# Global keys stored behind every third local key block of a windowed attention

## The chip, the core and the metric

The kernel runs on one core of one Trainium2 chip. The metric is the device time of one execution in microseconds (us), and less is better. The core has five engines with an instruction queue each: TensorE (PE, matrix products; its weight loads are listed apart as PEld), VectorE (DVE), ScalarE (ACT), GpSimd (POOL) and SyncE (SP). [...]

## The reference

Four batches of 8 heads have 512 local and 32 global tokens of width 64. A local query sees the 32 global keys and the local keys at most 32 places away; a global query sees everything. A dense squared-relu feed-forward layer and a layer of routed experts follow.

```python
k_all = np.concatenate([k_g, k_l], axis=2)
s_g = scale * np.matmul(q_g, k_all.transpose(0, 1, 3, 2))
out_g = np.matmul(sm(s_g), np.concatenate([v_g, v_l], axis=2))
s_ll = scale * np.matmul(q_l, k_l.transpose(0, 1, 3, 2))
mask = np.abs(pos[:, None] - pos[None, :]) <= 32
s_ll = np.where(mask, s_ll, -1000000000.0)
s_lg = scale * np.matmul(q_l, k_g.transpose(0, 1, 3, 2))
a_l = sm(np.concatenate([s_lg, s_ll], axis=-1))
out_l = np.matmul(a_l, np.concatenate([v_g, v_l], axis=2))
...
h = x @ w_in; r = np.maximum(h, 0.0); x2 = (r * r) @ w_out
# then: route each token of x2 to one of 8 experts, relu layer, gated sum
```

## The kernel before

**Stages.** The local queries are cut into 16 tiles t of 128 (tile t belongs to batch b = t // 4). `attention` (L392) makes one tile: scores, masked softmax, transposes, product with the values, transposition into the input of the feed-forward layer. `attention_global` (L478) makes the 32 global queries of a batch in two halves g of four heads. `ffn_block` runs the dense layer for two tiles at once (products h at L700 to L702, acc at L725 to L727; its first block works on plain, unsplit weights, L697 and L723). Then tokens are routed, and the expert layer fills the rest of the span.

**Order.** The order of the work is written out by hand in four strings of steps (`SEQ`, `EVEN`, `ODD`, `TAIL`); a letter stands for a step of a generator: `a` and `b` for attention tiles, `g` for global attention, `G` for the global keys, `0` to `3` for the key transposes of a head pair, `q` for queries, `E` and `F` for units of the dense layer, `V` for value loads, `W` for weight loads, `A` and `C` for conversions. Instructions of one engine run in the order in which the steps issue them.

**Keys.** `kT` of a batch holds the transposed keys of four head pairs, with the two heads of a pair in the two halves of 64 rows. `prep_k` (L326) makes four transposes for a head pair and one ACT copy (L331) of 128x512 elements into `kT`; `prep_globals` (L316) puts the 32 global keys behind the 512 local ones, in columns 512 to 543 (ACT copy, L320).

**Scores.** A tile is cut into four segments i of 32 queries. A segment sees a window of 96 local keys from `window(tt, i)` (L345) on, and the 32 global keys. So for a head pair p the loop at L404 makes, for both heads g, four products of 32 queries with 96 keys, and then four of 32 queries with 32 global keys: 64 products for a tile, all from L413. Each of the float32 products stands in the trace as two matmul records and two weight loads (128 records for a tile). The 4 segments write to the four quarters of 32 rows of the result, the 2 heads read the two halves of 64 rows.

**After the scores.** DVE adds one of three masks (L426; made by POOL at the start, L130 to L149, float32), takes the maximum, ACT makes the exponentials, PE transposes (L442), ACT or DVE copies, and PE multiplies with the value rows (`po`, L451). `load_v` (L353) fetches those rows: for each window one DMA for 96 local rows into rows 0 to 95 and one for the 32 global rows into rows 96 to 127. The first two tiles have places of their own (L369, L370), later windows rotate through six places `vr`, in which the global rows are loaded again only when the batch changes (L377, L380). All these DMAs are issued by SP.

**Global queries.** For each half, four products of 32 queries with 512 columns of `kT` (`gsa`) and four with 32 columns (`gsb`), L485.

Of the kernel before, what the change touches and what calls it, by code (L numbers as in the profile page):

```python
# [8 lines left out]
F32 = mybir.dt.float32  # L9
# [45 lines left out]
def attention_ffn_routed_experts(  # L55
# [73 lines left out]

    masks = {}  # L130
    for kind in range(3):
        m = const.tile([P, P], F32, name=f"mask{kind}")
        nc.gpsimd.memset(m, 0.0)
        for i in range(NQ):
            shift = 0
            if kind == 0 and i == 0:
                shift = SEG
            if kind == 2 and i == NQ - 1:
                shift = -SEG
            seg = m[SEG * i:SEG * (i + 1), 0:WIN]  # L140
            nc.gpsimd.affine_select(
                out=seg, in_=seg, compare_op=ALU.is_ge, fill=NEG,
                base=shift, pattern=[[1, WIN]], channel_multiplier=-1,
            )
            nc.gpsimd.affine_select(
                out=seg, in_=seg, compare_op=ALU.is_ge, fill=NEG,
                base=2 * SEG - shift, pattern=[[-1, WIN]], channel_multiplier=1,
            )
        masks[kind] = m  # L149
# [166 lines left out]
    def prep_globals(b):  # L316
        kT[b] = sb("kT", 1, [P, NPAIR, S], f"kT{b}")
        tr = pair(f"kgtr{b}")
        transposes(tr, kin[b, "g"][:, 0:DM], SG)
        nc.scalar.copy(kT[b][:, :, SL:S], tr[:, :, 0:SG])  # L320
        tr = pair(f"qgtr{b}")
        transposes(tr, kin[b, "g"][:, DM:2 * DM], SG)
        qgT[b] = sb("qgT", 1, [P, NPAIR, SG], f"qgT{b}")
        nc.scalar.copy(qgT[b], tr[:, :, 0:SG])

    def prep_k(b, p):  # L326
        tr = pair(f"ktr{b}_{p}")
        for j in range(TPB):
            two = kin[b, p // 2][:, j, 2 * (p % 2):2 * (p % 2) + 2, :]
            nc.tensor.transpose(tr[:, j, :], two.rearrange("p r d -> p (r d)"), ident)  # L330
        nc.scalar.copy(kT[b][:, p, 0:SL].rearrange("p (q j) -> p j q", j=TPB), tr)  # L331
# [13 lines left out]
    def window(tt, i):  # L345
        return min(max(tt * P + i * SEG - SEG, 0), SL - WIN)

    vin, vgl = {}, {}
    windows, opening, opening_places = [], [], []
    loaded = [0]  # L350
    globals_in = {}

    def load_v(t, part):  # L353
        if t >= NLT:
            return
        b, tt = divmod(t, TPB)
        for i in range(2 * part, 2 * part + 2):
            w0 = window(tt, i)
            if i and w0 == window(tt, i - 1):
                vin[t, i] = vin[t, i - 1]  # L360
                continue
            if t < 2:

                k, half = divmod(len(opening), 2)
                if half == 0:
                    opening_places.append(stage(f"v{k}"))
                w = opening_places[k][:, half * DM:(half + 1) * DM]
                opening.append(w)
                nc.sync.dma_start(heads(w[0:WIN]), v_l[b, :, w0:w0 + WIN, :].rearrange("h s d -> s h d"))  # L369
                nc.sync.dma_start(heads(w[WIN:P]), v_g[b].rearrange("h s d -> s h d"))  # L370
# [6 lines left out]
            nc.sync.dma_start(heads(windows[k][0:WIN]), v_l[b, :, w0:w0 + WIN, :].rearrange("h s d -> s h d"))  # L377
            if globals_in.get(k) != b:
                globals_in[k] = b
                nc.sync.dma_start(heads(windows[k][WIN:P]), v_g[b].rearrange("h s d -> s h d"))  # L380
            assert all(w is not windows[k] for w in vin.values())
            vin[t, i] = windows[k]
# [9 lines left out]
    def attention(t, S_TAG, O_TAG):  # L392
        b, tt = divmod(t, TPB)
        q = qT[t // 2][:, :, (t % 2) * P:(t % 2 + 1) * P]
        mask = masks[0 if tt == 0 else 2 if tt == TPB - 1 else 1]
# [10 lines left out]
        for p in range(NPAIR):  # L406
            for globals_ in (False, True):
                for i in range(NQ):
                    w0 = window(tt, i)
                    keys, cols = (slice(SL, S), slice(WIN, P)) if globals_ else (slice(w0, w0 + WIN), slice(0, WIN))  # L410
                    for g in range(2):
                        rows = slice(D * g, D * (g + 1))
                        nc.tensor.matmul(  # L413
                            scs[g][SEG * i:SEG * (i + 1), p, cols],
                            lhsT=q[rows, p, SEG * i:SEG * (i + 1)], rhs=kT[b][rows, p, keys],
                            start=True, stop=True,
                        )
# [4 lines left out]
        for g in range(2):  # L422
            if t != 1:
                sms[g] = sb("sm", 2, [P, S], f"sm{t}_{g}")[:, 0:4 * P]
# [53 lines left out]
    def attention_global(b, S_TAG, O_TAG):  # L478
        for g in range(2):
            sa = ps.tile([P, SL], F32, tag=S_TAG, bufs=BANKS[S_TAG], name=f"gsa{b}_{g}")  # L480
            sb_ = pair(f"gsb{b}_{g}")[:, 0, 0:SG]
            for o, c, n in ((sa, 0, SL), (sb_, SL, SG)):
                for hh in range(4):
                    p, r = divmod(4 * g + hh, 2)
                    nc.tensor.matmul(  # L485
                        o[SG * hh:SG * (hh + 1), :],
                        lhsT=qgT[b][D * r:D * (r + 1), p, :], rhs=kT[b][D * r:D * (r + 1), p, c:c + n],
                        start=True, stop=True,
                    )
# [5 lines left out]
            pg = sb("sm", 2, [P, S], f"pg{b}_{g}")  # L495
            rs = sb("osum", 2, [P, H], f"grs{b}_{g}")
            nc.scalar.activation(pg[:, 0:SL], sa, AF.Exp, bias=mx[:, 3:4], scale=SCALE, accum_out=rs[:, 0:1])
            nc.scalar.activation(pg[:, SL:S], sb_, AF.Exp, bias=mx[:, 3:4], scale=SCALE, accum_out=rs[:, 1:2])
# [5 lines left out]
            for c in range(TPB):  # L504
                nc.tensor.transpose(ptr[:, c, :], pg[:, 0:SL].rearrange("p (k j) -> p j k", j=TPB)[:, c], ident)
# [3 lines left out]
            nc.tensor.transpose(ptr[0:SG, 0, :], pg[:, SL:S], ident)  # L509
# [245 lines left out]
    def ffn_tile(t):  # L755
# [3 lines left out]
        place = sb("kT", 1, [P, NPAIR, S], f"g{t}").rearrange("p a s -> p (a s)")  # L759
# [181 lines left out]
    def wide_tile(e):  # L941
# [4 lines left out]
        def first(f):  # L946
# [8 lines left out]
            gl = sb("sm", 2, [P, S], f"ewgl_{e}_{f}")[:, 0:WIDE].bitcast(F32R)  # L955
# [23 lines left out]
        ys = sb("kT", 1, [P, NPAIR, S], f"ewys_{e}").rearrange("p a s -> p (a s)")[:, 0:KD * WIDE]  # L979
# [42 lines left out]
    def expert_tile(e, j, si):  # L1022
# [4 lines left out]
        hl = sb("kT", 1, [P, NPAIR, S], f"ehl_{name}").rearrange("p a s -> p (a s)")[:, 0:2 * KE * P].bitcast(F32R)  # L1027
# [8 lines left out]
        def first(fb, k0, k1):  # L1036
# [8 lines left out]
            if k1 == KD:  # L1045
                rs[fb] = sb("sm", 2, [P, S], f"er_{name}_{fb}")[:, 0:512]
                nc.scalar.activation(rs[fb], h, AF.Relu)
# [118 lines left out]
    def rest_tile(e, j, in_arm, o):  # L1166
# [13 lines left out]
        r = sb("sm", 2, [P, S], f"er_rest{e}")[:, 0:fw]  # L1180
# [31 lines left out]
    with tc.manual_schedule():  # L1212
# [48 lines left out]
        idle = sb("sm", 2, [P, S], "idle").bitcast(BF16)[:, 0:DM]  # L1261
# [50 lines left out]
        both = sb("kg", 1, [P, 2 * NSLOT], "slots", I32)  # L1312
# [96 lines left out]
        def more(e, j):  # L1409

            if j == UNROLL:
                with tc.For_i(UNROLL, (n_tok[e] + (P - 1)) // P, 1) as it:
                    gi = sb("gi", 2, [P, 1], f"gi{e}", I32)
# [190 lines left out]
```

## Time and profile before

| | us |
|---|---|
| median of 3 runs | 708.66 (707.76 to 709.51) |
| the profiled execution | 710.78 |
| its span in the trace | 709.1 |
| mean granted clock of TensorE | 0.98 |
| PE busy in the span | 683.5 (96%) |
| DVE / ACT / POOL busy | 396.2 / 365.5 / 163.7 |

The profiled execution is 2.1 us longer than the median, and 1.7 us of it lie outside the span. A row of the timeline is an engine's instructions of one form that run one after another: start, length, engine, line, tiles, shape and count; what stands in square brackets is the idle time before it and what ended that. The granted clock is a share: 1.00 is the higher of TensorE's two levels (2.4 GHz), 0.50 the lower (1.2 GHz).

### The profile page before, as it was taken

Reading aid. Unit: us, or ns where it says so; the run is one execution under the profiler, and the core shown is the slowest. Engines: PE = TensorE matmul, PEld = TensorE weight load, DVE = VectorE, ACT = ScalarE, POOL = GpSimd, SP = SyncE. Lnnn points to the kernel's source line nnn. Section 1 sums busy time; section 2 is a strip of 40 time slices with the busy share of each in tenths; the row PEclk is TensorE's granted clock in tenths of the full one; section 3 lists DMA queues with packets and bytes.
Section 4 is the critical chain, followed back from the end, with each engine's and each line's share of the span. In section 5 each row is a group of like instructions: output and inputs, shape, how many; then the busy total and the mean of one; then the engine's idle time right before and its main releaser. Section 6 shows DMA issues by size and latency. Waiting matters only on the chain. (4 is left out here: it accounts for less than half of the span.)

```text
span 709.1 us, 18592 instructions
## 1 busy us (share of the span) xinstructions
PE 683.5 (96%) x7621; PEld 574.3 (81%) x7621; DVE 396.2 (56%) x1073; ACT 365.5 (52%) x939; POOL 163.7 (23%) x205
## 2 busy tenths in 40 slices
PE   6789999999999999999999999999999999999996
PEld 4566668788888888988898888888887887898875
DVE  1879973873556166165516526544338733915984
ACT  5756557665535545453555545344434514515862
POOL 6000043354211121211221221122220432401311
PEclk8699999999999999999999999999999999999998
DMA  9999744056052501306350120410026588962920
GB/s 273 245 276 245 281 112 106 2 130 125 2 139 61 146 31 36 84 2 146 91 109 32 36 75 2 161 62 1 31 84 201 204 272 285 374 254 77 388 96 21
DMA packets 118758, 93.90 MB, mean 132 GB/s; under 512 B 84789, under 2 KB 91957, under 8 KB 118660
## 3 DMA queue, kind: packets, MB, share of 16 engines
q1 hardware_dynamic: 108352, 71.01, 35.9%
q10 hardware_dynamic: 8292, 15.48, 6.6%
q0 software_dynamic: 2016, 6.09, 2.5%
q8 instruction: 63, 1.03, 0.6%
q14 instruction: 35, 0.29, 0.1%
HBM read 80.31 MB, written 12.66 MB: 131 GB/s over the span
## 5 line engine op out<-in xcount | busy, mean ns | idle before, releaser
L184 POOL TENSOR_TENSOR gl<-g,gh 128x256 fp32r<-128x256 f32 x107 | 79.7, 745 | 302.8 <-ACT gh L183 142.3
L700 PE MATMUL h<-xh,w_in 128*128 128x256 f32 x464 | 134.9, 291 | 0.7 <-ACT xh L183 0.7
L701 PE MATMUL h<-xl,w_in 128*128 128x256 f32 x464 | 129.6, 279 | 0.3 <-DVE xl L184 0.3
L702 PE MATMUL h<-xh,w_in 128*128 128x256 f32 x464 | 129.7, 280 | 0.0
L725 PE MATMUL acc<-w_out,gh 128*128 128x512 f32 x232 | 97.5, 420 | 1.5 <-ACT gh L183 1.5
L727 PE MATMUL acc<-w_out,gl 128*128 128x512 f32 x232 | 91.9, 396 | 0.2
L726 PE MATMUL acc<-w_out,gh 128*128 128x512 f32 x232 | 91.6, 395 | 0.0
L700 PEld LDWEIGHTS h<-xh,w_in 128*128 128x128 f32 x464 | 87.1, 188 | 4.2 <-ACT xh L183 0.9
L704 ACT ACTIVATE g<-h 128x256 f32<-128x256 f32 x128 | 48.9, 382 | 78.9 <-PE h L702 45.0
L701 PEld LDWEIGHTS h<-xl,w_in 128*128 128x128 f32 x464 | 87.2, 188 | 2.6 <-DVE xl L184 0.5
L702 PEld LDWEIGHTS h<-xh,w_in 128*128 128x128 f32 x464 | 87.1, 188 | 0.1
L433 ACT ACTIVATE sm<-sm,mx 128x128 f32<-128x128 f32 x120 | 46.7, 390 | 48.3 <-DVE mx L431 48.3
L741 DVE TENSOR_TENSOR g<-h,g 128x256 f32<-128x256 f32 x53 | 22.2, 420 | 85.5 <-ACT g L704 85.4
L183 ACT CAST gh<-g 128x256 fp32r<-128x256 f32 x116 | 47.2, 407 | 42.4 <-DVE g L741 40.1
L727 PEld LDWEIGHTS acc<-w_out,gl 128*128 128x128 f32 x232 | 43.5, 188 | 11.9 <-POOL gl L184 1.5
L725 PEld LDWEIGHTS acc<-w_out,gh 128*128 128x128 f32 x232 | 43.6, 188 | 8.6 <-ACT gh L183 1.9
L726 PEld LDWEIGHTS acc<-w_out,gh 128*128 128x128 f32 x232 | 43.8, 189 | 5.7
L426 DVE TENSOR_TENSOR sm<-sc,mask 128x512 f32<-128x512 f32 x30 | 20.6, 688 | 24.5 <-PE sc L413 23.7
L255 POOL TENSOR_TENSOR w_in<-st_raw_in,w_in 128x512 fp32r<-128x512 f32 x10 | 13.0, 1309 | 83.1 <-ACT w_in L251 83.1
L743 ACT ACTIVATE g<-g 128x256 f32<-128x256 f32 x63 | 26.2, 416 | 5.1 <-ACT g L704 2.6
L413 PEld LDWEIGHTS sc<-kT,qT 64*32 64x32 f32 x2048 | 25.0, 109 | 4.3 <-issue 3.5
L413 PE MATMUL sc<-kT,qT 64*32 64x96 f32 (+1 forms) x2048 | 27.1, 229 | 0.1
(634 smaller groups left out, 1466.5 us busy)
## 6 DMA issues: line engine op xcount, KB each, us to landing
st_e<-in_moe_w_dram SPq DMA_DIRECT2D x46, 512.0 KB, 5.6
vr<-in_v_l_dram SPq DMA_DIRECT2D x49, 192.0 KB, 4.1
st_raw_in<-in_moe_w_in_dram SPq DMA_DIRECT2D x16, 512.0 KB, 8.1
st_raw_out<-in_moe_w_out_dram SPq DMA_DIRECT2D x16, 512.0 KB, 8.0
st_e<-in_moe_w_dram ACTq DMA_DIRECT2D x12, 512.0 KB, 5.3
x2d<-x ACTq DMA_DIRECT2D x19, 256.5 KB, 3.8
st_gv<-in_v_l_dram SPq DMA_DIRECT2D x8, 512.0 KB, 5.5
out_dram<-x ACTq DMA_DIRECT2D x16, 256.0 KB, 3.7
```

The costliest lines, as they stand in the source:

```text
L183: nc.scalar.copy(hi, src)
L184: (lo_engine or nc.vector).tensor_tensor(out=lo, in0=src, in1=hi.bitcast(F32), op=ALU.subtract)
L413: nc.tensor.matmul(scs[g][SEG * i:SEG * (i + 1), p, cols], lhsT=q[rows, p, SEG * i:SEG * (i + 1)], rhs=kT[b][rows, p, keys], start=True, s ...
L433: nc.scalar.activation(sm[:, hh, :], sm[:, hh, :], AF.Exp, bias=mx[:, hh:hh + 1], scale=SCALE, accum_out=osum[:, 2 * hh + g:2 * hh + g + 1],)
L700: nc.tensor.matmul(h, lhsT=wh, rhs=xh[:, k, :], start=(k == 0), stop=False)
L701: nc.tensor.matmul(h, lhsT=wh, rhs=xl[:, k, :], start=False, stop=False)
L702: nc.tensor.matmul(h, lhsT=wl, rhs=xh[:, k, :], start=False, stop=(k == KD - 1))
L704: nc.scalar.activation(g, h, AF.Relu)
L725: nc.tensor.matmul(acc[z], lhsT=gh[:, c], rhs=wh, start=first_one, stop=False)
L726: nc.tensor.matmul(acc[z], lhsT=gh[:, c], rhs=wl, start=False, stop=False)
L727: nc.tensor.matmul(acc[z], lhsT=gl[:, c], rhs=wh, start=False, stop=last_one)
L743: nc.scalar.activation(square, g, AF.Square)
```

## The change

The global keys are stored again and again between the local ones: the 16 local blocks of 32 keys lie in `kT` in threes, and behind every three come the 32 global keys, so that `kT` has 672 columns (5 groups of 128, and the last local block). Any three neighbouring local blocks then lie with one copy of the global keys in 128 columns that follow one another; where the copy lies among them depends on the window (`globals_at`). A segment's scores are one product over 128 columns. The masks (one for each tile of a batch, bfloat16, in the place that the slot tables use later) and the value rows have the same order. So the local value rows of a window come as two DMAs where the copy lies between them (two windows of three), and the key copies are two for a head pair: 5 groups of 24x4 keys, and the last block. For batch 0 the copy of the global keys and the last blocks are made by DVE, for the others by ACT.

```diff
+    def place(n):
+        return (n + n // 3) * SEG
+    def first_block(tt, i):
+        return min(max(tt * NQ + i - 1, 0), BLOCKS - 3)
+    def globals_at(w):
+        return (3 - w % 3) * SEG
...
-    for kind in range(3):
-        m = const.tile([P, P], F32, name=f"mask{kind}")
+    def make_mask(tt):
+        m = mask_place.bitcast(BF16)[:, tt * P:(tt + 1) * P]
...
-        nc.scalar.copy(kT[b][:, :, SL:S], tr[:, :, 0:SG])
+        put = nc.vector.tensor_copy if b == 0 else nc.scalar.copy
+        put(
+            kT[b][:, :, 0:KEYS - SEG].rearrange("p a (g c) -> p a g c", c=P)[:, :, :, WIN:P],
+            tr[:, :, 0:SG].unsqueeze(2).to_broadcast([P, NPAIR, KEYS // P, SG]),
+        )
...
-        nc.scalar.copy(kT[b][:, p, 0:SL].rearrange("p (q j) -> p j q", j=TPB), tr)
+        q = WIN * (KEYS // P) // TPB
+        nc.scalar.copy(
+            kT[b][:, p, 0:KEYS - SEG].rearrange("p (g q j) -> p j g q", j=TPB, q=P // TPB)[:, :, :, 0:WIN // TPB],
+            tr[:, :, 0:q].rearrange("p j (g q) -> p j g q", q=WIN // TPB),
+        )
+        put = nc.vector.tensor_copy if b == 0 else nc.scalar.copy
+        put(kT[b][:, p, KEYS - SEG:KEYS].rearrange("p (q j) -> p j q", j=TPB), tr[:, :, q:P])
...
+    def load_window(o, b, w):
+        at = globals_at(w)
+        for row, n, key in ((0, at, w * SEG), (at + SG, WIN - at, w * SEG + at)):
+            if n:
+                nc.sync.dma_start(heads(o[row:row + n]), v_l[b, :, key:key + n, :].rearrange("h s d -> s h d"))
...
-            if globals_in.get(k) != b:
-                globals_in[k] = b
+            if globals_in.get(k) != (b, at):
+                globals_in[k] = b, at
...
-            for globals_ in (False, True):
-                for i in range(NQ):
-                    w0 = window(tt, i)
-                    keys, cols = (slice(SL, S), slice(WIN, P)) if globals_ else (slice(w0, w0 + WIN), slice(0, WIN))
-                    for g in range(2):
-                        rows = slice(D * g, D * (g + 1))
-                        nc.tensor.matmul(
-                            scs[g][SEG * i:SEG * (i + 1), p, cols],
-                            lhsT=q[rows, p, SEG * i:SEG * (i + 1)], rhs=kT[b][rows, p, keys],
-                            start=True, stop=True,
-                        )
+            for i in range(NQ):
+                k0 = place(first_block(tt, i))
+                for g in range(2):
+                    rows = slice(D * g, D * (g + 1))
+                    nc.tensor.matmul(
+                        scs[g][SEG * i:SEG * (i + 1), p, :],
+                        lhsT=q[rows, p, SEG * i:SEG * (i + 1)], rhs=kT[b][rows, p, k0:k0 + P],
+                        start=True, stop=True,
+                    )
...
-            for o, c, n in ((sa, 0, SL), (sb_, SL, SG)):
+            for o, c in (
+                (threes, slice(0, most)), (sa[:, SL - SEG:SL], slice(most, KEYS)), (sb_, slice(WIN, P)),
+            ):
```

In the program, PE has 8106 rows instead of 8610, ACT 1193 instead of 1182, DVE 1488 instead of 1483, POOL 523 instead of 528 and SP 407 instead of 371.

On PE, the scores of the first tile begin behind the key transposes (`ktr`); `sc0_0` and `sc0_1` are the two heads' results. Before, where the wide products of the first head pair end and the narrow ones begin:

```order
L413 MATMUL sc0_1_274<-kT0_198,qT0_241 32x96
L413 MATMUL sc0_0_273<-kT0_198,qT0_241 32x96
L413 MATMUL sc0_1_274<-kT0_198,qT0_241 32x96
L413 MATMUL sc0_0_273<-kT0_198,qT0_241 32x32
L413 MATMUL sc0_1_274<-kT0_198,qT0_241 32x32
```

and now, at the beginning of the tile:

```order
L348 MATMUL ktr0_3_280<-ident_70,st_k0_1_207 128x128 x4
L440 MATMUL sc0_0_296<-kT0_217,qT0_263 32x128
L440 MATMUL sc0_1_297<-kT0_217,qT0_263 32x128
L440 MATMUL sc0_0_296<-kT0_217,qT0_263 32x128
L440 MATMUL sc0_1_297<-kT0_217,qT0_263 32x128
```

The 16 products of a head pair have become 8, so a tile has 32 instead of 64; what stands in front of and behind them is the same.

On ACT, the key copies of batch 1 among the conversions (`w_in`), the relu (`g`) and the rounding (`gh`, `xh`) that the dense layer waits for. Before:

```order
L331 COPY kT_1428<-ktr_0_1473 128x4x128
L251 CAST w_in_0_1479<-st_raw_in_0_256 128x512
L704 ACTIVATE g_15_1495<-h_15_1482 128x256
L331 COPY kT_1428<-ktr_1_1497 128x4x128
L331 COPY kT_1428<-ktr_2_1503 128x4x128
L183 CAST gh_15_1509<-g_15_1495 128x256
L183 CAST xh_957<-xtr_1520 128x4x128
```

and now:

```order
L350 COPY kT_1342<-ktr_0_1387 128x4x5x24
L355 COPY kT_1342<-ktr_0_1387 128x4x8
L265 CAST w_in_0_1394<-st_raw_in_0_278 128x512
L739 ACTIVATE g_15_1410<-h_15_1397 128x256
L350 COPY kT_1342<-ktr_1_1412 128x4x5x24
L355 COPY kT_1342<-ktr_1_1412 128x4x8
L350 COPY kT_1342<-ktr_2_1419 128x4x5x24
L355 COPY kT_1342<-ktr_2_1419 128x4x8
L197 CAST gh_15_1426<-g_15_1410 128x256
L197 CAST xh_861<-xtr_1437 128x4x128
```

Every key copy has a small one behind it, in front of what the dense layer waits for.

On SP, the value rows (`st_v`) of the first tiles, behind pieces of the weights (`st_raw_in`). Before:

```order
L209 DMA st_raw_in_3_0_270<-in_moe_w_in_dram 128x1024
L369 DMA st_v0_229<-in_v_l_dram 96x8x64
L370 DMA st_v0_229<-in_v_g_dram 32x8x64
L369 DMA st_v1_354<-in_v_l_dram 96x8x64
L370 DMA st_v1_354<-in_v_g_dram 32x8x64
```

and now:

```order
L223 DMA st_raw_in_3_0_293<-in_moe_w_in_dram 128x1024
L376 DMA st_v0_250<-in_v_l_dram 64x8x64
L376 DMA st_v0_250<-in_v_l_dram 32x8x64
L399 DMA st_v0_250<-in_v_g_dram 32x8x64
L376 DMA st_v1_346<-in_v_l_dram 32x8x64
L376 DMA st_v1_346<-in_v_l_dram 64x8x64
L399 DMA st_v1_346<-in_v_g_dram 32x8x64
```

The same bytes come with an issue more for a window whose copy of the global rows lies between its local rows; 36 windows of the whole program are of this kind, 9 in each batch.

## Rows read from the trace of the kernel before

**Rows 1.** The page, part 1: busy time of each engine, its share, instructions.

```profile
PE 683.5 (96%) x7621; PEld 574.3 (81%) x7621; DVE 396.2 (56%) x1073; ACT 365.5 (52%) x939; POOL 163.7 (23%) x205
```

**Rows 2.** Busy time by stretch: from:to, length, engines, clock, DMA share, GB/s.

```profile
20.00:40.00 20.00, 15.58 (x421) 12.20 (x422) 18.05 (x38) 13.32 (x42) 0.00 (x0) 0.69 1.00 260
...
100.00:140.00 40.00, 38.13 (x514) 33.16 (x514) 23.10 (x58) 28.00 (x79) 14.98 (x14) 1.00 0.28 61
180.00:300.00 120.00, 120.00 (x1621) 105.52 (x1620) 57.98 (x198) 59.50 (x185) 22.51 (x32) 1.00 0.30 73
```

**Rows 3.** PE's waits over the whole span: us in total, times, longest.

```profile
PE ptr L442 <- ACT st_sm L433: 3.2, 1, 3.2
PE h L697 <- issue: 2.8, 1, 2.8
PE ptr L442 <- ACT sm L433: 2.4, 1, 2.4
...
PE acc L725 <- ACT gh L183: 1.5, 2, 0.7
...
PE h L700 <- ACT xh L183: 0.7, 1, 0.7
```

**Rows 4.** PE's timeline around the scores of tiles 0, 1 and a later one.

```profile
14.48 1.85 PE L413 MATMUL sc<-kT,qT 64*32 64x96 f32 x128
...
20.26 2.69 PE L413 MATMUL sc<-kT,qT 64*32 64x96 f32 x128
...
44.70 0.49 PE L697 MATMUL h<-st_x,st_raw_in 128*128 128x256 f32 x1 [2.83 <-issue]
...
181.15 1.62 PE L413 MATMUL sc<-kT,qT 64*32 64x96 f32 x128
182.70 0.39 PE L700 MATMUL h<-xh,w_in 128*128 128x256 f32 x1
```

**Rows 5.** L413 alone, stretches of that later tile: PE, PEld, clock, DMA.

```profile
181.14:181.20 0.06, 0.05 (x8) 0.05 (x12) 1.00 0.00 0
...
181.14:181.42 0.28, 0.27 (x32) 0.27 (x33) 1.00 0.00 0
...
181.14:182.20 1.06, 1.05 (x96) 1.05 (x101) 1.00 0.00 0
181.14:182.60 1.46, 1.45 (x128) 1.45 (x128) 1.00 0.00 0
```

**Rows 6.** PE's timeline around products of 512 and of 64 columns.

```profile
193.59 1.06 PE L485 MATMUL gsa<-kT,qgT 64*32 64x512 f32 x8
194.47 0.24 PE L485 MATMUL gsb<-kT,qgT 64*32 64x32 f32 x8
...
198.87 1.10 PE L451 MATMUL po<-vr,pT 128*32 128x64 f32 x64
199.90 0.39 PE L505 MATMUL gptr<-ident,pg 128*128 128x128 f32 x1
```

**Rows 7.** ACT's copies by line (ns least/median/most), and one timeline row.

```profile
L331 ACT COPY kT<-ktr x16: 1065/1092/1147, 9.1 to 372.0; 128x512 f32<-128x512 f32 x16
...
L320 ACT COPY kT<-kgtr x4: 266/266/272, 7.6 to 362.4; 128x128 f32<-128x128 f32 x4
...
L444 ACT COPY pT<-ptr x8: 558/567/596, 23.9 to 73.6; 128x512 f32<-128x512 f32 x8
...
110.19 2.01 ACT L331 COPY kT<-ktr 128x512 f32<-128x512 f32 x2
```

**Rows 8.** Timeline: the last masks on POOL, their first use on DVE.

```profile
9.35 1.00 POOL L145 TENSOR_SCALAR_AFFINE_SELECT mask<-mask 32x96 f32<-32x96 f32 x2
...
16.50 0.69 DVE L426 TENSOR_TENSOR sm<-sc,mask 128x512 f32<-128x512 f32 x1 [2.49 <-PE sc L413]
```

**Rows 9.** SP's timeline: issues of value rows, the longest and the shortest.

```profile
13.62 2.52 SPq L370 DMA_DIRECT2D st_v<-in_v_g_dram  x1
...
20.62 0.54 SPq L370 DMA_DIRECT2D st_v<-in_v_g_dram  x1
```

More of the change, by code (lines that the diff above doesn't have):

```diff
@@ L128, in attention_ffn_routed_experts @@
     make_identity(nc, ident)
+    BLOCKS = SL // SEG
+    KEYS = (BLOCKS + (BLOCKS - 1) // 3) * SEG
+    def place(n):
[4 more added lines that the diff above has]
+        return (3 - w % 3) * SEG
     masks = {}
-    for kind in range(3):
-        m = const.tile([P, P], F32, name=f"mask{kind}")
+    mask_place = const.tile([P, 2 * NSLOT], I32, name="masks_slots")
+    def make_mask(tt):
+        m = mask_place.bitcast(BF16)[:, tt * P:(tt + 1) * P]
         nc.gpsimd.memset(m, 0.0)
         for i in range(NQ):
[L135 to L143, printed above, removed]
-            )
[L145 to L149, printed above, removed]
+            w = first_block(tt, i)
+            for n in range(3):
+                away = w + n - (tt * NQ + i)
+                seg = m[SEG * i:SEG * (i + 1), place(w + n) - place(w):place(w + n) - place(w) + SEG]
+                if abs(away) > 1:
+                    nc.gpsimd.memset(seg, NEG)
+                elif away:
+                    nc.gpsimd.affine_select(
+                        out=seg, in_=seg, compare_op=ALU.is_ge, fill=NEG,
+                        base=0, pattern=[[-away, SEG]], channel_multiplier=away,
+                    )
+        masks[tt] = m
+    for tt in range(TPB):
+        make_mask(tt)
     iota_s = const.tile([P, NSLOT], F32, name="iota_s")
@@ L357, in load_v @@
         for i in range(2 * part, 2 * part + 2):
-            w0 = window(tt, i)
-            if i and w0 == window(tt, i - 1):
+            w0 = first_block(tt, i)
+            at = globals_at(w0)
+            if i and w0 == first_block(tt, i - 1):
                 vin[t, i] = vin[t, i - 1]
@@ L394, in attention @@
         q = qT[t // 2][:, :, (t % 2) * P:(t % 2 + 1) * P]
-        mask = masks[0 if tt == 0 else 2 if tt == TPB - 1 else 1]
+        mask = masks[tt]
         osum = sb("osum", 2, [P, H], f"osum{t}")
@@ L481, in attention_global @@
             sb_ = pair(f"gsb{b}_{g}")[:, 0, 0:SG]
[L482 removed]
+            most = KEYS - SEG
+            threes = sa[:, 0:SL - SEG].rearrange("p (g c) -> p g c", c=WIN)
+            for o, c in (
+                (threes, slice(0, most)), (sa[:, SL - SEG:SL], slice(most, KEYS)), (sb_, slice(WIN, P)),
+            ):
                 for hh in range(4):
                     p, r = divmod(4 * g + hh, 2)
+                    keys = kT[b][D * r:D * (r + 1), p, c]
+                    if o is threes:
+                        keys = keys.rearrange("p (g c) -> p g c", c=P)[:, :, 0:WIN]
                     nc.tensor.matmul(
[L486 to L487 removed]
+                        o[SG * hh:SG * (hh + 1)],
+                        lhsT=qgT[b][D * r:D * (r + 1), p, :], rhs=keys,
                         start=True, stop=True,
@@ L1258, in do @@
                 emits[j](what[1:])
-        idle = sb("sm", 2, [P, S], "idle").bitcast(BF16)[:, 0:DM]
+        idle = sb("sm", 2, [P, SL], "idle").bitcast(BF16)[:, 0:DM]
         nc.vector.memset(idle, 0.0)
@@ L1310, in attention_ffn_routed_experts @@
                     emit(what)
-        both = sb("kg", 1, [P, 2 * NSLOT], "slots", I32)
+        both = mask_place
         gidx, sidx = both[:, 0:NSLOT], both[:, NSLOT:2 * NSLOT]
```

42 lines of the change are left out of this document (20 added, 22 removed).

## The prediction

> **What bounds the kernel now.** I read the busy times first: PE is busy for 96% of the span, the next engine, DVE, for 56% [rows 1]. An average over stages hides who is late where, so I took the stretches next. From 180 us on PE is busy for 120.00 of 120.00 us at full clock, while DVE and ACT have less than half of their time in use and the DMA share is 0.30 [rows 2]: there every microsecond that PE saves moves all that follows. From 100 to 140 us PE is at 38.13 of 40.00, with ACT at 28.00 [rows 2]: a saving of PE counts there, and so does a lengthening of ACT. From 20 to 40 us the DMA engines are full (share 1.00), PE has 15.58 of 20.00 and a granted clock of 0.69 [rows 2]: PE's products are not what is late. Last the list of PE's waits. Those of 3.2 and 2.4 us are the softmaxes of the first two tiles, one is 2.8 us in which PE waited for nothing that the profile shows, and the rest are below a microsecond each [rows 3].
>
> **The scores, the main term.** A tile's 128 records begin at 181.15 and the next product begins at 182.70 [rows 4]: 1.55 us. Two tiles ran at a lower clock, tiles 0 and 1; the other 14 are like this one. What sets these 1.55 us? The first 8 records begin within 0.06 us, so two row halves and four quarters do run together, and the first 32, which are one head pair with both widths, begin within 0.28 us. After that the pace falls: 64 more records need 1.06 - 0.28 = 0.78 us, 0.39 us for a head pair [rows 5]. A head pair streams 2 passes of 96 and 2 of 32 columns in either case, 256 columns when 8 products run together; if columns were the limit, the second pair would be as fast as the first. So I read the 0.39 us as the pace at which 16 products with their 16 weight changes come, 24 ns for a product, and the 0.28 us as what the columns need.
>
> After the change a head pair has 8 products, which at 24 ns come in 0.20 us, and still 256 columns. The columns now decide. Their price has two neighbours with the same 1024 columns that a tile has: two passes of 512 take 194.47 - 193.59 = 0.88 us, and sixteen passes of 64 take 199.90 - 198.87 = 1.03 us [rows 6]. Eight passes of 128 lie between, 0.88 + 6/14 x 0.15 = 0.94 us. The other end is four times the first head pair's 0.28 us, 1.12 us. I take the middle, 1.04 us, since the score products run over two row halves at a time as those of 512 columns do, but change weights as often as those of 64. The saving is 0.51 us for a tile, between 0.43 and 0.61.
>
> Twelve tiles lie behind 100 us: 12 x 0.51 = 6.1 us. Tiles 2 and 3 lie before that, where the DMA engines are full; I count half, 0.5 us for the two, with ends of 0 and 1.2. Tiles 0 and 1 take 1.85 and 2.69 us [rows 4], but the softmax waits behind them are 2.4 and 3.2 us [rows 3], and the first product's result can reach DVE only when the last is done; what they save (at most 1 us) is counted at nothing, since what follows waits for weights that the full DMA engines bring.
>
> **Global queries.** Four products of 512 and four of 32 columns become four of 480, four of 32 and four of 32, in two row halves: the columns are the same, and four more small products at 24 ns are 0.1 us at most for each of eight halves, against 32 columns less in the long ones. 0, with ends of -0.2 and +0.8 us.
>
> **ACT's copies.** A key copy takes 1.09 us for 512 elements [rows 7]; for 480 it is 0.07 us shorter, if length counts in proportion. Behind it comes a copy of 32 elements. No row shows one; the nearest is the copy of 128 elements, 0.27 us [rows 7], which I take as its price; 0 would be the other end. Net +0.20 us for a head pair, and 12 of them on ACT in batches 1 to 3. The copy of the global keys grows from 128 to 640 elements: 0.57 x 640/512 = 0.71 us by the plain copy, 1.09 x 640/512 = 1.37 us by the key copy [rows 7], so +0.4 to +1.1 us, three times. In the steady stretch ACT is idle half the time [rows 2] and nothing of this is seen. Batch 1 is the exception: two of its key copies (2.01 us from 110.19 on, [rows 7]) stand directly in front of the rounding for which PE then waits 0.7 us [rows 3]. There both small copies count: +0.4 us, with ends of 0 and +1.1, the latter if the global copy is also late. In batch 0 these copies are DVE's.
>
> **DVE and POOL.** DVE's five new copies lie before the first mask addition, for which it has 2.49 us of idle time directly ahead [rows 8]: 0 to +0.5 us. POOL has 30 small selections instead of 24 wide ones; at the 0.5 us each that two take 1.00 us for [rows 8] this is at most +3 us, and the masks end at 10.35 now with their first use at 16.50, so it is covered. That the masks are bfloat16 lets DVE's addition stay at its length; if it grew it would be covered by DVE's idle half [rows 2].
>
> **SP and the transfers.** Nine more issues in the first 64 us, 36 in all; the bytes are the same. One issue takes 0.54 to 2.52 us [rows 9] when the queue is full. Since the DMA engines have a share of 1.00 there [rows 2], SP's length is a sign of their load and not the limit. 0, with ends of -0.5 and +2 us; the larger case is a rival below. In later batches the DMA share of 0.30 covers them.
>
> **The sum.** -6.1 (twelve tiles) -0.5 (two tiles) +0.4 (ACT) = -6.2 us. The profiled execution of 710.78 us becomes 704.6; the median of the runs stands 2.1 us lower, so 708.66 becomes 702.5 us. The ends: with 0.61 us for a tile, 1.2 for tiles 2 and 3 and no cost it is 12 x 0.61 + 1.2 = 8.5 less, 700.2; with 0.43, nothing for tiles 2 and 3, +1.1 on ACT and +0.8 for the global queries it is 3.3 less, 705.4.
>
> **The rivals.** *The stall goes.* The 2.83 us at 44.70 [rows 4] in which PE waited for nothing shown come behind a long run of small instructions, with the DMA engines full. If it is the fetch of PE's instructions, 512 products with two records each fewer may move it to where it is covered: 702.5 - 2.8 = 699.7. Against it: the bytes that fill the DMA engines are unchanged, and some fetch must fall somewhere. Chance 0.15.
>
> *The pace is not that of the products.* The 0.39 us for a head pair may come from the columns after all (the first pair being quick because its operands had been made ready), or the 128 columns start slower for another reason. Half the way gives 1.30 us for a tile: 12 x 0.25 = 3.0, -0.4 on ACT, 706.1 at the middle and 709 with no saving. For it: the ends of matmuls are modelled, and two row halves share one stream of keys. Against it: 0.86 ns for a column at 512 columns [rows 6] against 1.5 at 0.39 us for 256. Chance 0.13.
>
> *ACT reaches the path.* If ACT's extra work shows in all three batches: 12 x 0.20 + 3 x 0.43 = 3.7 us instead of 0.4, 705.8. Against it PE's waits for ACT, which are 1.5 us in two pieces and 0.7 us in one [rows 3]. Chance 0.05.
>
> *Slower: SP's queue sets the pace of the opening.* If value rows or weights land late because SP issues late, nine issues at the mean of the two rows, 1.53 us, come on the path: +13.8, 716.3 us. It decides as soon as the DMA engines are no longer full between 20 and 40 us; a share of 1.00 [rows 2] is against it. Chance 0.06.
>
> *Slower: products of one row half don't run together at 128 columns.* Then the 16 products of a half, two passes each of 0.94/8 = 0.12 us, run in a row: 3.8 us for a tile, 12 x (3.8 - 1.04) = 33 us more than forecast, 735 us. Eight records begun in 0.06 us, four from each half, speak against it [rows 5]. Chance 0.03. The Trainium skill, page "TensorE: Matmul & The Clock Gate", Part 3, "What overlaps and what doesn't", states that a weight load overlaps matmuls in flight only when the row group differs; by that the four segments of a head would follow one another and the tile would come out as in this rival. The trace does not agree: 12 weight loads and 8 matmuls begin within 0.06 us over only two row groups.
>
> That the products are not merged at all is excluded by the program's rows, which show 32x128.
>
> **How the numbers follow.** The forecast has 0.58. About 0.3% of the time, 2.1 us, is what a measurement of this kernel can tell from no change. Faster by more: the forecast, the stall, 0.09 of the pace and 0.03 of ACT, 0.85. Within: 0.04 of the pace and 0.02 of ACT, 0.06. Slower: 0.09. The range goes from 698.5 (the stall with a little more for the tiles) to 706.5 (ACT, or half of the pace); it leaves out the slower cases, the worst of the pace and the best of the stall with the best tiles, some 0.17.
>
> **What would show it.** In the trace after, a later tile's scores should last 1.04 us from their first record to the next product, with 64 records; above 1.25 the pace rival holds, above 2 the last one. PE should still have no waits from 180 us on. PE's wait for `xh` near 110 us should be some 0.4 us longer, and the 2.8 us of issue should be there near 45 us; if it is gone, the time is below 700. If PE waits for a value or weight DMA before 65 us with the DMA share below 0.95, SP is the cause. The small ACT copies should be at or below 0.28 us.

## The result, and the profile after

The changed kernel takes 702.68 us (median of 6 runs, 701.72 to 703.07) against 709.09 us (median of 6 runs, 707.33 to 712.92): a ratio of 0.9904, with a 95% interval of 0.9878 to 0.9931. Forecast were 702.5 us and a range of 698.5 to 706.5. The profiled execution took 702.01 us with a span of 700.3 us, 8.8 us less than the span of before; the medians differ by 6.4. That gap is taken up below.

Busy times and two stretches of the changed kernel (columns as in [rows 1, 2]):

```profile
PE 674.1 (96%) x6661; PEld 563.4 (80%) x6661; DVE 395.9 (57%) x1078; ACT 365.7 (52%) x950; POOL 164.3 (23%) x214
...
100.00:140.00 40.00, 37.35 (x375) 31.73 (x374) 23.23 (x58) 29.37 (x83) 16.64 (x16) 1.00 0.25 58
...
180.00:300.00 120.00, 120.00 (x1395) 104.99 (x1394) 58.38 (x202) 60.88 (x192) 23.53 (x32) 1.00 0.30 73
```

PE has 960 records less, and is still busy for all of 180 to 300 us: the bound is the same engine. PE's timeline around the scores of the same later tile as in [rows 4], then L440 alone from their start (columns as in [rows 5]):

```profile
177.26 1.16 PE L440 MATMUL sc<-kT,qT 64*32 64x128 f32 x64
178.35 0.39 PE L735 MATMUL h<-xh,w_in 128*128 128x256 f32 x1
...
177.25:177.31 0.06, 0.05 (x7) 0.05 (x11) 1.00 0.00 0
177.25:177.53 0.28, 0.27 (x20) 0.27 (x28) 1.00 0.00 0
177.25:178.08 0.83, 0.82 (x59) 0.82 (x64) 1.00 0.00 0
```

The scores last 178.35 - 177.26 = 1.09 us instead of 1.55. The pace is now even: 39 records between 0.28 and 0.83 us, 14 ns each. Eight products of 128 columns (16 records) so take 0.23 us, 0.88 ns for a column, which is the price of the 512-column products (0.86, [rows 6]). The columns decide, as forecast.

PE's waits of the changed kernel, whole span, and three rows of its timeline:

```profile
PE ptr L469 <- ACT st_sm L460: 3.9, 1, 3.9
PE ptr L469 <- ACT sm L460: 2.8, 2, 2.4
...
PE acc L758 <- ACT gh L778: 0.8, 1, 0.8
PE ktr L348 <- DVE kT L335: 0.7, 1, 0.7
...
PE h L735 <- ACT xh L197: 0.7, 1, 0.7
PE ktr L348 <- DVE kT L355: 0.5, 1, 0.5
PE qtr L365 <- DVE kT L355: 0.5, 1, 0.5
...
15.39 1.67 PE L440 MATMUL sc<-kT,qT 64*32 64x128 f32 x64
...
43.93 2.07 PE L758 MATMUL acc<-st_raw_out,gh 128*128 128x512 f32 x4 [0.79 <-ACT gh L778]
...
109.46 0.38 PE L735 MATMUL h<-xh,w_in 128*128 128x256 f32 x1 [0.68 <-ACT xh L197]
```

Against [rows 3]: the wait for nothing shown (2.8 us) is not there; a wait of 0.8 us for ACT stands in its neighbourhood; PE waits three times for DVE's new copies in the opening, and the first scores begin at 15.39 instead of 14.48 us (in a second profile of the kernel before, experiment 11, at 15.42); the wait for `xh` near 110 us is as long as before.

**Where the 8.8 us of the two profiles lie.** Each of the tiles 2 to 15 is 0.46 us shorter: 14 x 0.46 = 6.4. At the start of tile 2 the changed kernel is 0.26 us late (37.06 instead of 36.80). From the end of those scores to the start of tile 3 it gains 2.84 us (from 38.15 to 48.10, instead of from 38.35 to 51.14): that is the stall (the wait of 2.83 us for nothing that the profile shows), and the lower clock behind it, less the new wait. Three rows of before, and a stretch of the changed kernel:

```profile
45.46 3.21 PE L723 MATMUL acc<-st_raw_out,gh 128*128 128x512 f32 x4
...
51.14 1.62 PE L413 MATMUL sc<-kT,qT 64*32 64x96 f32 x128
...
45.00:50.00 5.00, 5.00 (x17) 2.98 (x16) 2.79 (x6) 4.01 (x13) 0.00 (x0) 0.66 0.83 296
...
40.00:60.00 20.00, 19.04 (x191) 12.62 (x190) 18.86 (x38) 14.92 (x45) 0.00 (x0) 1.00 1.12 285
```

In the kernel before, after 2.83 us without work four products took 3.21 us at a granted clock of 0.66 (in part 2.4, in part 1.2 GHz), and the same four 2.07 us in the changed kernel, which shows 1.00 there. Between the scores of tiles 5 and 6, 0.6 us is given back (tile 5 ends 4.5 us earlier than before, tile 6 starts 3.9 us earlier), and 0.4 us is gained in small pieces elsewhere: -6.4 + 0.26 - 2.84 + 0.6 - 0.4 = -8.8.

### The profile page after: what moved, and what is told of

Same layout as the page of the kernel before. It is cut to its first block, busy times and chain, and to the rows that moved or that the text cites. A ratio compares the mean times of both kernels' runs of the same rounds, so it can differ in the third digit from the quotient of the medians.

```text
span 700.3 us, 16768 instructions
## 1 busy us (share of the span) xinstructions
PE 674.1 (96%) x6661; PEld 563.4 (80%) x6661; DVE 395.9 (57%) x1078; ACT 365.7 (52%) x950; POOL 164.3 (23%) x214
## 5 line engine op out<-in xcount | busy, mean ns | idle before, releaser
L776 DVE TENSOR_TENSOR g<-h,g 128x256 f32<-128x256 f32 x53 | 22.2, 419 | 85.9 <-ACT g L739 85.8
L453 DVE TENSOR_TENSOR sm<-sc,masks_slots 128x512 f32<-128x512 f32 x30 | 20.6, 688 | 15.3 <-PE sc L440 14.2
L758 PE MATMUL acc<-st_raw_out,gh 128*128 128x512 f32 x48 | 23.9, 618 | 0.8 <-ACT gh L778 0.8
L469 PE MATMUL ptr<-ident,sm 128*128 128x128 f32 x120 | 20.3, 281 | 3.4 <-ACT sm L460 2.8
```

The source lines that it names most:

```text
L758: nc.tensor.matmul(acc[z], lhsT=gh[:, c], rhs=w, start=first_one, stop=last_one)
```

## Experiments

**1. The products cut again, all else as changed.**

```diff
-            for i in range(NQ):
-                k0 = place(first_block(tt, i))
-                for g in range(2):
...
-                        scs[g][SEG * i:SEG * (i + 1), p, :],
-                        lhsT=q[rows, p, SEG * i:SEG * (i + 1)], rhs=kT[b][rows, p, k0:k0 + P],
+            for c0, c1 in ((0, 96), (96, 128)):
+                for i in range(NQ):
+                    k0 = place(first_block(tt, i))
+                    for g in range(2):
...
+                            scs[g][SEG * i:SEG * (i + 1), p, c0:c1],
+                            lhsT=q[rows, p, SEG * i:SEG * (i + 1)], rhs=kT[b][rows, p, k0 + c0:k0 + c1],
```

> The changed kernel with one thing undone: each product of 128 columns is cut again into one of 96 and one of 32, in the order of before (first the wide ones of a head pair, then the narrow ones). Layout, masks, key copies and value loads stay those of the change. Theory (the scores are held up by the number of products, and the rest of the change costs next to nothing): a later tile's scores last 1.55 us again instead of 1.09, the time is that of the kernel before within 1 us, 708 to 710 us. Rival (the gain has another source, the vanished stall of 2.8 us near 45 us or the new layout): the scores may be long again, but the time stays below 706 us. On the stall: if it is the fetch of instructions and hangs on how many PE has, a wait of PE for nothing shown of 1 us or more is back between 30 and 60 us.

Measured: 710.20 us, ratio to the kernel before 1.0018 (0.9998 to 1.0038). PE's timeline of this kernel, in three places:

```profile
44.51 0.49 PE L733 MATMUL h<-st_x,st_raw_in 128*128 128x256 f32 x1 [1.56 <-issue]
...
52.35 0.42 PE L441 MATMUL sc<-kT,qT 64*32 64x96 f32 x21 [1.50 <-issue]
...
181.23 1.62 PE L441 MATMUL sc<-kT,qT 64*32 64x96 f32 x128
182.79 0.39 PE L736 MATMUL h<-xh,w_in 128*128 128x256 f32 x1
```

The scores last 1.56 us again, and the whole gain is gone: merging the products is worth all of it. The time lies 1.3 us above that of the kernel before, -0.1 to +2.7 by the interval: that bounds what else the change does (copies, masks, 36 more DMA issues). The stall is back as well, in front of the same product, with a second one in the scores of tile 3, which may be part of the 1.3 us; so this run alone doesn't part what the shorter scores bring from what the missing stalls bring. The stretches do: 6.4 us come from the fourteen tiles.

**2 and 3. Equal halves, and quarters.** The same edit with other cuts:

```diff
-            for c0, c1 in ((0, 96), (96, 128)):
+            for c0, c1 in ((0, 64), (64, 128)):
...
-            for c0, c1 in ((0, 96), (96, 128)):
+            for c0, c1 in ((0, 32), (32, 64), (64, 96), (96, 128)):
```

> The changed kernel with each product of 128 columns cut into two of 64: 64 products for a tile as before, but of equal width. Theory (24 ns for a product, whatever its width): 0.39 us for a head pair behind the first, a later tile's scores 1.50 to 1.60 us, time as with 96 and 32, 708 to 710 us. Rival (the narrow products of 32 columns are what was slow, since a product has a shortest time that 32 columns don't fill): with 64 columns the scores last 1.1 to 1.3 us and the time is 703 to 706 us.

Measured: 709.49 us, ratio 0.9996 (0.9977 to 1.0016).

> The changed kernel with each product of 128 columns cut into four of 32: 128 products for a tile, the same columns. Theory (24 ns for a product): a tile's scores last 128 x 24 ns = 3.0 us (2.8 to 3.2), 1.9 us more than with the change, 14 tiles: 702.7 + 27 = 729 us (726 to 732). Rival (the pace is that of the columns or of the change of form): the scores last 1.1 to 1.6 us and the time is below 712 us.

Measured: 777.71 us, ratio 1.0921 (1.0866 to 1.0977), 48 us above the theory. PE's timeline with halves (one tile), then with quarters (one tile), and the first of PE's waits with quarters:

```profile
181.81 1.48 PE L441 MATMUL sc<-kT,qT 64*32 64x64 f32 x128
183.23 0.39 PE L736 MATMUL h<-xh,w_in 128*128 128x256 f32 x1
```

```profile
241.30 1.72 PE L441 MATMUL sc<-kT,qT 64*32 64x32 f32 x144
244.06 1.28 PE L441 MATMUL sc<-kT,qT 64*32 64x32 f32 x112 [1.04 <-issue]
...
PE sc L441 <- issue: 39.1, 17, 4.9
```

With halves a tile takes 1.42 us, a little under the 1.50 to 1.60 of the theory and above the 1.1 to 1.3 of its rival: it is the number of products that costs, and the width has a small part in it. With quarters the tile shown lasts 1.72 + 1.28 us without its wait, 3.0 us for 128 products, 23 ns each, as forecast. But waits for nothing that the profile shows come on top, 39.1 us in 17 places, also behind 100 us where the DMA engines are mostly idle. The theory had left out what brings the instructions (experiments 8 to 10). Some 9 of the 48 us are not accounted for; the mean granted clock is 0.96 here instead of 0.98 to 0.99.

**4. The cut value loads alone**, in the kernel before.

```diff
+    def load_window(o, b, w0):
+        at = (3 - w0 // SEG % 3) * SEG
+        for r0, r1 in ((0, at), (at, WIN)):
+            if r0 < r1:
+                nc.sync.dma_start(heads(o[r0:r1]), v_l[b, :, w0 + r0:w0 + r1, :].rearrange("h s d -> s h d"))
...
-                nc.sync.dma_start(heads(w[0:WIN]), v_l[b, :, w0:w0 + WIN, :].rearrange("h s d -> s h d"))
+                load_window(w, b, w0)
```

> The kernel before with one part of the change alone: the local rows of a value window come as two DMAs where the changed kernel cuts them (36 more issues on SP, the same bytes and places). Theory (the DMA engines set the pace of the opening, not SP's queue): no difference, ratio 0.998 to 1.003. Rival (SP's queue is late in the first 64 us): nine issues at 0.5 to 1.5 us, 4 to 14 us slower.

Measured: 709.60 us, ratio 1.0012 (0.9995 to 1.0029). The 4 us of the rival are excluded; a cost of up to 2 us is not.

**5. One row half after the other.**

```diff
-            for i in range(NQ):
-                k0 = place(first_block(tt, i))
-                for g in range(2):
+            for g in range(2):
+                for i in range(NQ):
+                    k0 = place(first_block(tt, i))
```

> The changed kernel with the two inner loops of the scores exchanged: for a head pair the four segments of the first row half, then the four of the second, instead of the halves in turn. Same products, same number. If what matters is only that eight products of a head pair run together, and the order doesn't: a later tile's scores stay at 1.09 us and the time at 702.7 us within 1. If products of one row half hold each other up (a weight load waits for the matmuls of its half, as the last rival of the prediction has it), neighbours in the order no longer overlap: 1.5 us or more for a tile, 708 us or more.

Measured: 702.11 us, ratio 0.9904 (0.9880 to 0.9927); the same later tile and the product behind it:

```profile
177.71 1.16 PE L440 MATMUL sc<-kT,qT 64*32 64x128 f32 x64
178.80 0.39 PE L735 MATMUL h<-xh,w_in 128*128 128x256 f32 x1
```

1.09 us in either order. Neighbours that load weights into the same row half do not hold each other up here. The rule of the Trainium skill that the prediction cites ("TensorE: Matmul & The Clock Gate", Part 3, "What overlaps and what doesn't") would have had them do so.

**6. The new copies on ACT in batch 0 as well.**

```diff
-        put = nc.vector.tensor_copy if b == 0 else nc.scalar.copy
+        put = nc.scalar.copy
```

> The changed kernel with the copies of batch 0's global keys and last key blocks on ACT, as in the other batches, instead of DVE. In the changed kernel's opening PE waits for those DVE copies (0.7 and 0.5 us) and the first scores begin at 15.39 instead of 14.48 us. If that wait is on the path to the end, ACT's version moves the time by as much as the first scores move: ACT has five more copies (some 1.9 us) in its chain, so 0.5 to 1.5 us slower, 703 to 704. If the opening is set by the weights that the DMA engines bring, the first scores move and the time does not: 702.7 within 0.7.

Measured: 701.83 us, ratio 0.9905 (0.9888 to 0.9922). The first scores begin at 15.01 us, and the time is 0.85 us lower than that of the changed kernel, so neither 0.5 to 1.5 us more nor 702.7 us within 0.7 came out. The two ratios to the kernel before are the same to 0.0001, so nothing says that this version is better.

**7. The new copies on DVE in all batches.**

```diff
-        put = nc.vector.tensor_copy if b == 0 else nc.scalar.copy
+        put = nc.vector.tensor_copy
```

> The changed kernel with the copies of the global keys and of the last key blocks on DVE in all batches, which takes 15 copies away from ACT behind 100 us. The prediction charged 0.4 us for two of them in batch 1. The trace after shows PE's wait for the rounding near 110 us unchanged (0.68 us), so the theory now is that they cost nothing: 702.7 within 0.7 us. Rival: they cost their 0.4 us or more elsewhere, 702.3 us or less, which needs more than these rounds to be told; a time above 703.5 would say that DVE is the worse place.

Measured: 702.62 us, ratio 0.9922 (0.9903 to 0.9941): no difference to the changed kernel. PE's wait for `xh` near 110 us:

```profile
109.37 0.38 PE L735 MATMUL h<-xh,w_in 128*128 128x256 f32 x1 [1.20 <-ACT xh L197]
```

It is longer (1.20 us) without ACT's small copies than with them (0.68). DVE is the cause. Its product `g` (L776) now comes behind a small copy that had to wait for ACT's key copy, and ACT waits 0.59 us for `g` before it can round (DVE's rows, then ACT's):

```profile
107.87 0.21 DVE L355 COPY kT<-ktr 128x32 f32<-128x32 f32 x1 [0.66 <-ACT kT L350]
107.98 0.41 DVE L776 TENSOR_TENSOR g<-h,g 128x256 f32<-128x256 f32 x1
...
108.42 0.40 ACT L197 CAST gh<-g 128x256 fp32r<-128x256 f32 x1 [0.59 <-DVE g L776]
```

So this wait doesn't say what the copies cost on ACT. ACT's timeline in the changed kernel does:

```profile
106.54 1.03 ACT L350 COPY kT<-ktr 128x480 f32<-128x480 f32 x1
107.35 0.28 ACT L355 COPY kT<-ktr 128x32 f32<-128x32 f32 x1
107.41 1.10 ACT L350 COPY kT<-ktr 128x480 f32<-128x480 f32 x1
108.27 0.30 ACT L355 COPY kT<-ktr 128x32 f32<-128x32 f32 x1
108.33 0.46 ACT L197 CAST gh<-g 128x256 fp32r<-128x256 f32 x1
```

A small copy lasts 0.28 us from its start to its end, but the next instruction starts 0.06 us after it. From the first key copy to `gh` are 108.33 - 106.54 = 1.79 us with four copies, and 111.98 - 110.19 = 1.79 us with two in the kernel before (`gh` begins there at 111.98), so the small copies were no burden on ACT:

```profile
111.98 0.43 ACT L183 CAST gh<-g 128x256 fp32r<-128x256 f32 x1
```

**8 to 10. Is the stall the fetch of PE's instructions?** The page's row of the instruction queue (packets, MB, share), before, after, and with quarters:

```profile
q8 instruction: 63, 1.03, 0.6%
```

```profile
q8 instruction: 55, 0.90, 0.5%
```

```profile
q8 instruction: 79, 1.29, 0.7%
```

Experiment 1 has 63 packets too. It has 512 products more than the changed kernel, with two matmuls and two weight loads each: 2048 instructions and 8 packets, 256 instructions for a packet, or 128 records of PE with their weight loads. The quarters add 4096 to the 63 packets of experiment 1, and 16 packets: the same. (The count of packets is good to one: the changed kernel profiled again shows 56.) If PE stops where such a packet ends, a shift of half a packet must move the stall, and a shift of a whole one must leave it in its place in the program. Tiny products were put behind the warm-up, with the kernel before (64, then 128) and with the changed one (64):

```diff
         for _ in range(n):
             nc.tensor.matmul(o, lhsT=idle[:, 0:P], rhs=idle, start=True, stop=True)
+        for _ in range(64):
+            nc.tensor.matmul(o[0:SEG, 0:SEG], lhsT=idle[:, 0:SEG], rhs=idle[:, 0:SEG], start=True, stop=True)
```

> The kernel before with 64 tiny products of 32 columns more on PE behind the eight warm-up products, while PE waits for its first keys anyway: 128 instructions more in the queue, half of the 256 that one of the 16 KB packets of the instruction queue holds. Theory (the wait for nothing shown near 45 us is the fetch of PE's instructions, which comes at a fixed count): it stands again before the same record in PE's count (behind 599 records, now 64 places earlier in the program), that is inside the scores of tile 2 instead of the dense layer's product L697, or is hidden there. Rival (the stall belongs to that product, for its weights or its bank): it stays in front of the sixteenth product of L697. Time: that of the kernel before within 2 us either way.

Measured: 717.04 us, ratio 1.0118 (1.0089 to 1.0147). PE's timeline at three places:

```profile
20.94 0.35 PE L413 MATMUL sc<-kT,qT 64*32 64x32 f32 x11 [5.13 <-issue]
...
43.86 0.66 PE L413 MATMUL sc<-kT,qT 64*32 64x96 f32 x49 [1.42 <-issue]
...
57.58 0.54 PE L451 MATMUL po<-vr,pT 128*32 128x64 f32 x24 [1.80 <-issue]
```

PE alone, from the start of the span to the stall (from:to, length, busy time and records): the kernel before; with 64 tiny products, at its first and its second stall; with 128; and experiment 1, at its first and its second:

```profile
0.00:44.65 44.65, 30.74 (x599) 0.77 1.01 252
```

```profile
0.00:20.90 20.90, 12.94 (x221) 0.91 1.01 256
0.00:43.80 43.80, 27.21 (x599) 0.81 1.02 257
```

```profile
0.00:43.30 43.30, 31.77 (x727) 0.84 1.01 264
```

```profile
0.00:44.40 44.40, 30.73 (x599) 0.88 0.99 253
0.00:52.30 52.30, 37.08 (x727) 0.90 0.99 270
```

With 64 tiny products the stall left the dense layer's product and stands in the scores of tile 2, again behind exactly 599 records. New ones came in the scores of tile 0 (5.13 us, behind 221 records) and in the value products near 57 us. Between 599 and 727 lie 128 records. Between 221 and 599 lie 378, which are 756 instructions with their weight loads, and 12 semaphore instructions of PE: 768, three times 256. Counted so, all 34 waits of PE for nothing shown in the 14 profiles, 18 of them in the one with quarters, stand behind 450 instructions plus a multiple of 256, within 2. And the packets of the instruction queue are in the trace with their times: the one in front of the 2.83 us of the kernel before came in from 41.97 to 43.35 us, 1.34 us before PE went on. All the 34 waits but one of 0.17 us ended 1.2 to 1.7 us behind the end of such a packet. The expectation on the time (within 2 us) was wrong: half a packet of instructions that do nothing costs 8 us.

> The kernel before with 128 tiny products more, 256 instructions or one whole packet of the instruction queue. If the stalls lie at borders of such packets, a whole packet more puts every border back where it was in the program: the wait of some 2 us stands again in front of the sixteenth product of L697 (record 727 of PE instead of 599), the 5 us in the scores of tile 0 are gone, and the time is that of the kernel before within 2 us, plus what the tiny products take beyond PE's idle time (at most 1.5 us). If the 64 tiny products cost their 8 us for another reason (the warm-up, the clock, PE late at its first keys), 128 of them cost as much or more: 716 us or more.

Measured: 709.62 us, ratio 1.0020 (1.0008 to 1.0033). Its stall:

```profile
43.32 0.49 PE L697 MATMUL h<-st_x,st_raw_in 128*128 128x256 f32 x1 [1.73 <-issue]
```

Twice the tiny products cost 1 us instead of 8, and the stall is in its old place in the program, behind 727 records: 599 and one packet of 128. Warm-up, clock and a late start are excluded as causes; PE waits for its instructions, at packet borders, where small products have used them up quickly.

> The changed kernel with the same 64 tiny products more behind the warm-up. If PE stops at fixed counts of its instructions while the DMA engines are full (every 128 records with their weight loads, as 221, 599 and 852 of the kernel before with the tiny products suggest), the border that lay in the value products of tile 0 near 30 us now lies in the scores of tile 1 near 21 us, and a wait for nothing shown of 1 to 5 us may stand there, in front of record 215 to 221; the time is then 704 to 709 us, and part of the gain of the change hangs on where its instructions happen to lie. If the changed kernel, with half the score instructions, is no longer open to that, the time stays at 702.7 within 1.

Measured: 702.61 us, ratio 0.9918 (0.9897 to 0.9939). PE shows no wait for nothing in this profile. With half the instructions in the scores, the changed kernel did not stop at the shifted border.

**11 and 12. Both kernels profiled once more.**

> The kernel before as it is, profiled once more. The first pair of profiles differs by 8.8 us in span, the medians of the runs by some 6.3. If the difference lies in how long PE's wait for its instructions happens to be (2.8 us in the first profile of before, 1.6 to 1.7 us at the same record in the profiles with the scores cut and with the value loads alone), the wait stands again in front of record 600 (behind 599), shorter, near 1.7 us, and the span is 706 to 708 us. If it is 2.8 us again and the span 709, the first profile was a usual one and the medians need another explanation.

> The changed kernel as it is, profiled once more, beside the repeated kernel before. Expected: no wait for nothing shown, a later tile's scores 1.09 us, the first scores at 15 us within 0.7, and a span of 700 to 702 us. A span above 703, or a stall, would say that the changed kernel scatters as the one before does.

Measured: a span of 708.5 us (one run, 710.25 us) and of 699.0 us (700.66 us). PE's wait for nothing in the repeated kernel before:

```profile
PE h L697 <- issue: 2.8, 1, 2.8
```

So 2.8 us it is again, and the expectation of 1.7 us fell. The changed kernel has no such wait again; its first scores begin at 15.70 us, and its span is 1.0 us below the range expected. Two more rows of the repeated kernel before, the first scores and the four products behind its stall:

```profile
15.42 1.97 PE L413 MATMUL sc<-kT,qT 64*32 64x96 f32 x128
...
46.06 1.97 PE L723 MATMUL acc<-st_raw_out,gh 128*128 128x512 f32 x4
```

Those four took 1.97 us, not 3.21: the lower clock did not follow the same stall here. Of the 9.5 us by which the second pair of profiles differs, the fourteen tiles give the same 6.4; the stall gives 1.2, a second one of 0.49 us in the scores of tile 3 (again a packet border) 0.8, the opening nothing, and 0.9 lie behind the last scores. Why the medians differ by less (6.4 us) stays open: the two profiled executions of the kernel before (710.78 and 710.25 us) lie 1.2 to 2.2 us above its medians of 708.58 to 709.09, those of the changed kernel 0.7 and 2.0 us below its own, and how long PE stalls in an execution without a profile was not seen. Where the profiled stall was shorter, 1.7 us at the same product (experiments 4 and 10), the spans were 706.6 and 705.4 us, against 709.1 and 708.5 with 2.8; the ordinary runs of the kernel before have a median span near 707. A shorter stall in most of them would explain the medians, but that is not shown.

## Why the prediction was right, step by step

- **The bound.** Right where it matters: PE has no wait from 180 to 420 us in either kernel, and behind that both have the same four, of 0.2 to 0.5 us. The saving of each of the tiles 2 to 15 is still there at the end.
- **The scores.** The mechanism was right: the number of products set the old pace, the columns set the new one. The size was 0.46 us for a tile instead of 0.51 (1.09 instead of 1.04 us), inside the bounds of 0.43 to 0.61. The 0.28 us of the first head pair were not purely what its columns need: with quarters the first 32 records, with half of the columns, begin within 0.24 us too. Twelve tiles give 5.5 instead of 6.1 us. Tiles 2 and 3, counted at half, give it in full (0.9 instead of 0.5 us). Together 6.4 instead of 6.6.
- **ACT, mis-sized.** +0.4 us were charged, 0 was measured: the price of a small copy was read from its duration, and what the queue pays is the distance from start to start, 0.06 us. The copy of the global keys took 0.69 us, just below the 0.71 to 1.37.
- **DVE in the opening.** Counted at 0 to 0.5 us by DVE's idle time, with no word on who waits for the copies. PE did, three times (0.7, 0.5 and 0.5 us). The first scores were 0.9 us late in the first pair of profiles and 0.3 us in the second, for the opening of the kernel before scatters as well: its first transposes waited 2.1 us for POOL in the one profile and 2.8 us for a DMA in the other (when the prediction called the other waits shorter than a microsecond, it passed over the first). Of the 0.9 us, 0.7 were still there at the second softmax of tile 1 (27.91 instead of 27.20 us); behind it PE did not have the waits for value rows (0.25 and 0.50 us) of the first profile of before. So 0.26 us was left at tile 2, and nothing in the second pair: the copies cost next to nothing, but for another reason than the one given.
- **SP's loads.** No cost of several us (experiment 4), as forecast.
- **The stall: the step that failed.** It was taken as unchanged, with 0.15 for the rival that it goes. It went, in every profile of the changed kernel and of its variants with merged scores, and experiment 1 brought it back: 2.84 us in the first pair of profiles, with the low clock behind it, and 1.2 in the second, without. The rival's reason, the fetch of PE's instructions, was right (experiments 8 to 10); its price (699.7 us) is not what the medians show. That the forecast of 702.5 lies so close to 702.68 is therefore in part luck: by the profiles, from which its terms were taken, the kernel gained 8.8 and 9.5 us, by the medians 6.4, and a sum that had included the stall would have given some 700.
- **The other rivals.** The pace by columns (706.1 to 709) is excluded by the 1.09 us, ACT on the path by the unchanged wait of 0.68 us, SP's queue by experiment 4, and products of one row half that hold each other up by experiment 5.

## What to carry to other kernels

Many small matmuls that run together are paid by their number (23 ns each here) until one pass over the columns costs more: compare the pace at the start of the burst with the pace behind it, and merge products until both are equal, though it takes copies of data to make operands lie side by side. On an engine that takes one instruction after another, read the price of a small instruction from the distance between two starts, not from its duration. A wait that the profile can't explain, in front of an ordinary instruction behind a burst of small ones, may be the fetch of instructions: count the engine's instructions up to it (weight loads and semaphore instructions too), look when a packet of the instruction queue came in, and shift the count by a few cheap instructions before the place itself is blamed.

## What was not expected of the hardware

- PE's instructions come in packets of 16 KB, 256 instructions (63 packets in experiment 1 against 55 for 2048 instructions less). PE stopped at packet borders for up to 5.1 us in the opening, and with 128 products to a tile 17 times over the whole kernel, for 39.1 us in all.
- 64 tiny products in PE's idle time cost 8 us, 128 of them 1 us: where the borders fall decides.
- Two ACT copies of 480 and 32 elements follow one another in the time of one of 512 (1.79 us for two such pairs, and for two whole copies).
